# Loading the first batch's q in three long-row parts and putting the tokens back in order later

## The chip, the cores and the metric

The kernel runs on one core of one Trainium2 chip. The metric is the device time of one execution in microseconds (us); the runs before have a median of 262.91 us (three runs, 262.56 to 263.26). The core's engines are PE (TensorE, with its weight loads shown apart as PEld), DVE (VectorE), ACT (ScalarE), POOL (GpSimd) and SP, which here only issues DMAs. Each engine works through its own list of instructions in order and waits on semaphores for the others.

## The reference

There are two blocks, one after the other. The first is a linear attention over sketched features, for 4 batches, 4 heads, 1088 tokens and 32 dimensions:

```python
def phi(x):
    a = np.einsum('rd,bhsd->bhsr', S1, x)          # r = 8
    b = np.einsum('rd,bhsd->bhsr', S2, x)
    return np.einsum('bhsi,bhsj->bhsij', a, b).reshape(*x.shape[:-1], r * r)
q_p, k_p = (phi(q), phi(k))
kv = np.einsum('bhsf,bhsd->bhfd', k_p, v)
z = np.sum(k_p, axis=2)
num = np.einsum('bhsf,bhfd->bhsd', q_p, kv)
den = np.einsum('bhsf,bhf->bhs', q_p, z)[..., None] + 1e-06
attn_out = num / den                               # -> x[b, token, 128], heads side by side
```

The second is a mixture of 4 attention experts over x. A gate picks the best two experts of each token (`w_gate`), each expert does causal attention with its own `wq`, `wk`, `wv`, `wo` (64 wide), and the two results are added with softmax weights of the gate.

Two things matter for the change. The sums `kv` and `z` run over all tokens, so the order of k and v is free as long as both have the same one. q is different: row s of `num` belongs to token s, and the second block is causal, so x has to stand in token order.

## The kernel before

**An order written out by hand.** The kernel declares about 1,280 jobs (`job(...)`), each with the engines it may run on, what it reads and makes, and the buffers that it holds. `ORDER` is one list of job numbers; a letter picks one of two engines (`b` for the second), and a choice of "-" drops the job (unused dummies). `Plan.run` emits the jobs in this order, so each engine's instructions and each DMA queue come in this order, and buffers of a pool are handed out as the list goes: a job that takes a buffer waits until the buffer's former users are through. PSUM has four buffers of two banks, `pair0` to `pair3`, for all work of TensorE. The numbers of estimated microseconds in the jobs don't act at run time.

**The first batch's front.** `prepare(0, ...)` and `attend_rows` make x of batch 0; the later batches go through `attend_turned`, in the shadow of the batch before them.

- k and v of batch 0 come in long rows: partition (head, t) gets 34 adjacent tokens, t counts 32 of them (`load_k`, `load_v`). SP and ACT issue half of k each; SP issues v in four parts.
- q of batch 0 comes by head (`by_head`, line 436): four loads, two on SP and two on ACT. Partition t of a head holds the tokens t, 32 + t, 64 + t and so on, so each piece of a row is one token of 128 bytes. Column block c of 32 columns holds the tokens 32c to 32c + 31.
- DVE turns 32 x 32 blocks (`turn_k` line 484/488, `turn_q` line 494, q in pieces of 384 and 704 columns), so that the dimensions lie on partitions. Both pieces of q wait for all four loads.
- TensorE multiplies 128 tokens at a time with the sketch table `SD` (`project`, line 562); `low` (a copy by ACT or DVE, line 193 as all copies) and `lift` (DVE, line 574) join the two parts of the result, and `multiply` (DVE or POOL, line 580) forms the 64 feature products of each head.
- `spread v` (ACT and POOL, line 193) sets v beside a column of ones. `sums` (TensorE, line 619) adds k's features times v over all tokens, and `keep sums` (ACT) copies the result.
- `turn qf` (`turn_features`, TensorE, line 666) transposes q's features, 18 blocks of 128 x 128 in four jobs of 6, 4, 4 and 4 blocks, each into its own pair. `keep qf` (`keep_features`, ACT, line 193, `fp<-pair`) copies each to `qpT`, in the order in which it stands in PSUM.
- `numer` (TensorE, line 692) multiplies 64 tokens at a time with the sums, `divide` (DVE, lines 699 to 701) divides, `turn x` (TensorE, line 707) and `keep x` (ACT) give x with its 128 columns on partitions.
- `sketch k1` (TensorE, line 523) is the beginning of batch 1 and stands between the numerators.

Then follow the gate (`logits` line 884, `turn logits` line 888, `choose a` and `choose b` lines 911 to 927, `turn choice`, `widen`, masks by DMA through DRAM for the later groups of tokens), the queries (line 1066), `base` (ACT) and `pick` (DVE, line 1079), and the scores (line 1104), which `take` (DVE), `exp` (ACT), `weigh` (POOL) and `turn A` (DVE) pass on to the sums over values (line 1180). `features k1` (line 537) are products of batch 1 on POOL or DVE.

**Dummies.** Pairs of matmuls on a zero tile (line 250) keep TensorE busy before there is work; seven such jobs are in the list.

The lines that the change touches most, as they are:

```python
for y in range(y0, y1):
    z = y - y0
    nc.tensor.transpose(plan[t][:, z // w, 128 * (z % w) : 128 * (z % w) + 128], f[:, y], ident)
...
copy(e, plan[qpT][:, 128 * y0 : 128 * y1], plan[t][:, 0, 0 : 128 * (y1 - y0)])
```

Block y holds the features of two heads (y % 2) for the 128 tokens y // 2.

Of the kernel before, what the change touches and what calls it, by code (L numbers as in the profile page):

```python
# [21 lines left out]
0 1 2 3 4 78 79 83 15a 80 45 21a 48 46 10a 81 90 53b 52b 91 54b 50 25b 18a 49 55b 5b 12a 14a 51 82 84 87 85 86 94 64  # L22
63 95b 96 27a 57 56 58 92 99 93 98b 100a 65 104 97a 101 400 89b 66a 108 103a 88a 105a 114 68 69 106 102b 70 109a 401
115 71a 110 116a 117a 107a 113a 402 399 118 124 111a 112a 59 60 120 61 406 119a 410 125a 122 405 121a 126 67 403 409
127 413 123a 414 128 408 415 134 129a 130 62 407 135 154 131 72 74 73 75 417a 419a 132 155 77 133a 136 404 137a 412
160 161 418a 140 187 138 162 163 156 158 170 188 76 157 693 192a 159 171 175 47 164 165a 176 692 191a 416a 166 189
167a 178 190 691 145 421 177 420 193 141 694 194 411 195 196 197 179 216 230 209 217 182 172 701 422a 183 218 231 198a
424 423 425 428a 223 139 219a 202 173 232 210 233a 427b 184 199 220 174a 221 180 426b 211 702 429 224 203 234 253 222
212b 254 213 185 258a 326 41b 257a 181 431 144 39b 225 255 204 235 186a 256 153 28b 236 430 200 214 226b 215 432 327
149 143 330a 331a 259 205a 142 227 329 700 438 228 168 260 433 148 332 201 328 268 698 229 206 169a 276 434 275 24b  # L30
439 207 283 699 333 277 284 208 269 261 435a 278 270 300 299 285 262 286 436a 287a 237 440 696 279b 442a 437 301 238
9b 705 695 280 441a 288 263 443 264a 708 706 302 152 281 239 303b 240a 271b 241a 289 242a 272 444 709a 282 265 304 245
244 445a 290 704 359 358 712a 273 351 446a 274 350 305 306 707a 266 147 243a 292 710a 366 713a 360 291 367 26b 267 352
361 293 369 362a 11b 353 342 343 38b 294 711a 987 246 697 151 368 363 370 464 295a 296 297 344 345 714 715 371 298 465
# [81 lines left out]
def kernel(  # L116
# [14 lines left out]
    nc = tc.nc  # L131
# [291 lines left out]
    def prepare(b, rank):  # L423
# [42 lines left out]
        if early:  # L466
            for x in range(H):
                job(f"load q{b}.{x}", ("SP", "ACT")[x % 2], 0.7, lambda e, x=x: by_head(nc.scalar if e == "ACT" else nc.sync, plan[qin], q, x),
                    lead, ("qin", b, 0), [qin], landing=0.95, rank=-198.5)
# [921 lines left out]
```

## Time and profile before

| What | us |
|---|---|
| Median of three runs | 262.91 |
| The profiled execution, as timed | 263.49 |
| Its span in the profile | 261.8 |
| PE busy | 254.9 |
| DVE busy | 208.4 |
| POOL busy | 157.5 |
| ACT busy | 105.6 |

All times in the profile count from the start of the span. The profile is of one execution; it is timed 1.7 us longer than its span, and 0.58 us above the median of the runs shown. A row of the timeline gives start, duration of the group, engine, line, operation, what it writes and reads, how many, and in brackets the idle time of its engine before it with what ended it. Busy time of PE includes the dummies, and its matmuls overlap, so differences between starts tell better than durations how long a group holds the engine. TensorE multiplies float32 in two passes, each of which is one row of the count; a transpose is one pass. The granted clock of TensorE was full throughout.

### The profile page before, as it was taken

Reading aid. Unit: us, or ns where it says so; the run is one execution under the profiler, and the core shown is the slowest. Engines: PE = TensorE matmul, PEld = TensorE weight load, DVE = VectorE, ACT = ScalarE, POOL = GpSimd, SP = SyncE. Lnnn points to the kernel's source line nnn. Section 1 sums busy time; section 2 is a strip of 40 time slices with the busy share of each in tenths; the row PEclk is TensorE's granted clock in tenths of the full one; section 3 lists DMA queues with packets and bytes.
Section 4 is the critical chain, followed back from the end, with each engine's and each line's share of the span. In section 5 each row is a group of like instructions: output and inputs, shape, how many; then the busy total and the mean of one; then the engine's idle time right before and its main releaser. Section 6 shows DMA issues by size and latency. Waiting matters only on the chain.

```text
span 261.8 us, 9228 instructions
## 1 busy us (share of the span) xinstructions
PE 254.9 (97%) x3811; PEld 192.2 (73%) x3811; DVE 208.4 (80%) x529; ACT 105.6 (40%) x279; POOL 157.5 (60%) x266
## 2 busy tenths in 40 slices
PE   7899999999999999999999999999999999999995
PEld 2787666646958887665897986666689875589994
DVE  5778999999998996998887497998994388893442
ACT  3453354757242225532814044635514215723120
POOL 5546776899578716597467682366273842542642
PEclk9999999999999999999999999999999999999999
DMA  7978689891467275906044685003370379240012
GB/s 149 212 122 186 112 207 168 158 146 20 73 135 166 67 184 114 148 4 183 3 84 83 143 167 120 4 3 90 93 120 4 96 141 238 47 96 3 5 30 59
DMA packets 87739, 27.35 MB, mean 104 GB/s; under 512 B 58576, under 2 KB 87056, under 8 KB 87696
## 3 DMA queue, kind: packets, MB, share of 16 engines
q1 hardware_dynamic: 85184, 26.15, 50.7%
q10 hardware_dynamic: 2512, 0.61, 1.0%
q8 instruction: 30, 0.49, 0.8%
q14 instruction: 13, 0.11, 0.2%
HBM read 22.22 MB, written 4.52 MB: 102 GB/s over the span
## 4 chain that ended last, share of the span: by engine, by line
PE 84%; DMA 8%; DVE 5%; POOL 1%; issue 1%; SPq 0%; ACT 0%; DVEq 0%; POOLq 0%; ACTq 0%
PE pair L1180 28%; PE pair L1104 24%; PE pair L1066 9%; PE pair L1301 7%; DMA mb<-md 4%; PE pair L1251 3%; PE pair L523 2%; PE pair L827 2%; DMA in<-in_q_dram 2%; DMA w<-in_v_dram 2%; PE pair L627 2%; DVE w L1116 1%; PE pair L1277 1%; DVE fp L805 1%; PE pair L619 1%; PE pair L692 1%
## 5 line engine op out<-in xcount | busy, mean ns | idle before, releaser
L1147 POOL TENSOR_SCALAR w<-w,rs,sh 128x256 f32<-128x256 f32 (+14 forms) x68 | 56.8, 840 | 34.4 <-DVE rs L1143 32.8
L1104 PE MATMUL pair<-xT,qs 128*128 128x320 f32 (+9 forms) x216 | 74.0, 478 | 0.4 <-DVE qs L1079 0.4
L1132 ACT ACTIVATE w<-w,mx 128x64 f32<-128x64 f32 (+15 forms) x68 | 52.4, 772 | 45.8 <-DVE mx L1116 40.6
L1116 DVE CUSTOM_DVE_ANT_0 w<-pair,mask 128x64 f32<-128x64 f32 (+14 forms) x68 | 48.3, 723 | 15.4 <-PE pair L1104 13.0
L1104 PEld LDWEIGHTS pair<-xT,qs 128*128 128x128 f32 x216 | 38.8, 190 | 25.9 <-issue 11.1
L1152 DVE STREAM_TRANSPOSE AT<-w 128x320 f32<-128x320 f32 (+15 forms) x68 | 51.2, 762 | 3.4 <-POOL w L1147 3.0
L1180 PEld LDWEIGHTS pair<-AT,xra 32*128 32x128 f32 x1136 | 41.6, 185 | 4.6 <-issue 2.0
L1180 PE MATMUL pair<-AT,xra 32*128 32x160 f32 (+5 forms) x1136 | 44.9, 303 | 0.0
L1207 POOL TENSOR_TENSOR agg<-agg,mb 128x768 f32<-128x768 f32 (+1 forms) x22 | 34.0, 1559 | 3.4 <-DVE agg L1203 2.0
L1066 PE MATMUL pair<-xT,Mq 128*128 128x384 f32 (+1 forms) x96 | 34.0, 475 | 0.0
L193 ACT COPY agg<-pair 128x384 f32<-128x384 f32 (+1 forms) x31 | 13.2, 463 | 45.5 <-PE pair L1180 44.0
L1180 PEld LDWEIGHTS pair<-AT,xrb 32*128 32x128 f32 x752 | 26.4, 185 | 2.4 <-issue 2.2
L1180 PE MATMUL pair<-AT,xrb 32*128 32x160 f32 (+5 forms) x752 | 28.0, 289 | 0.0
L1140 POOL TENSOR_SCALAR rs<-zs 128x1 f32<-128x1 f32 x32 | 6.8, 214 | 34.0 <-ACT w L1132 23.5
L1066 PEld LDWEIGHTS pair<-xT,Mq 128*128 128x128 f32 x96 | 17.3, 190 | 10.3 <-issue 3.2
L1079 DVE COPY_PREDICATED qs<-mb,pair 128x768 f32<-128x768 uint16 (+1 forms) x24 | 23.1, 962 | 1.5 <-ACT qs L193 0.3
L537 POOL TENSOR_TENSOR fp<-w 128x576 f32<-128x576 f32 x19 | 22.6, 1209 | 1.6 <-DVE w L527 1.1
L1301 PEld LDWEIGHTS pair<-Mo,agg 128*128 128x128 f32 x168 | 20.6, 192 | 2.4 <-issue 0.5
L1301 PE MATMUL pair<-Mo,agg 128*128 128x128 f32 x168 | 21.4, 277 | 0.0
L193 ACT COPY qs<-pair 128x384 f32<-128x384 f32 (+1 forms) x21 | 9.2, 463 | 19.5 <-PE pair L1066 14.2
L1203 DVE COPY_PREDICATED agg<-mb,pair 128x384 f32<-128x384 uint16 (+1 forms) x24 | 12.7, 557 | 4.8 <-ACT agg L193 4.4
L1132 ACT ACTIVATION_READ_ACCUMULATOR w<-w,mx 128x1 f32 x68 | 12.8, 189 | 0.0
(179 smaller groups left out, 297.2 us busy)
## 6 DMA issues: line engine op xcount, KB each, us to landing
xra<-xd SPq DMA_DIRECT2D x16, 192.0 KB, 5.2
xrb<-xd SPq DMA_DIRECT2D x16, 192.0 KB, 5.4
xrc<-xd SPq DMA_DIRECT2D x16, 160.0 KB, 5.0
mb<-md SPq DMA_DIRECT2D x4, 576.0 KB, 7.4
mb<-md SPq DMA_DIRECT2D x4, 480.0 KB, 4.4
mb<-md SPq DMA_DIRECT2D x6, 288.0 KB, 4.3
in<-in_k_dram SPq DMA_DIRECT2D x12, 136.0 KB, 3.4
in<-in_q_dram SPq DMA_DIRECT2D x3, 544.0 KB, 5.6
```

Of the source, the lines that this page charges most:

```text
L193: (nc.scalar.copy if eng == "ACT" else VEC[eng].tensor_copy)(o, i)
L537: VEC[e].tensor_tensor(out=f, in0=a[:, :, None, R : 2 * R].to_broadcast([128, j1 - j0, R, R]), in1=a[:, :, 0:R, None].to_broadcast([128, j ...
L1066: nc.tensor.matmul(plan[ps[x]][:, y, 0:w], Mq[:, ((1, 2), (0, 3))[x][y]], plan[xT][:, 64 * t0 : 64 * t1], start=True, stop=True)
L1079: nc.vector.copy_predicated(chosen(), rows(c), rows(plan[ps[x]]))
L1104: nc.tensor.matmul(plan[p][:, y, 0 : c1 - c0], plan[qs][:, 128 * t : 128 * t + 128], plan[xT][:, c0:c1], start=True, stop=True)
L1116: nc.vector.tensor_tensor_reduce(out=o, in0=src, in1=msk, scale=-1.0, scalar=mx[:, b, i, x - 1 : x] if x else 3e38, op0=ALU.add, op1=ALU.m ...
L1132: nc.scalar.activation(out=a, in_=a, func=ACTF.Exp, bias=mx[:, b, i, last : last + 1], scale=-1.0, accum_out=zs[:, b, i : i + 1])
L1147: nc.gpsimd.tensor_scalar(out=a, in0=a, scalar1=rs[:, b, i : i + 1], scalar2=plan[("sh", b)][:, i : i + 1], op0=ALU.mult, op1=ALU.mult)
L1152: nc.vector.transpose(dst[:, 0 : keys // 32, t], plan[A][:, 0:keys].rearrange("p (j s) -> p j s", s=32))
L1180: nc.tensor.matmul(plan[Vk[g // 2]][:, g % 2, lo : 32 * nt], plan[(f"xr{j // 12}", b)][rows, j % 12], a[rows, j, lo:], start=(j == 0), sto ...
L1207: nc.gpsimd.tensor_tensor(out=a, in0=a, in1=plan[mb][:, 2 * x : 2 * x + 2, 0:w], op=ALU.mult)
L1301: nc.tensor.matmul(plan[p][0:m, 0, 128 * x : 128 * x + 128], plan[agg][:, e, 128 * x : 128 * x + m], Mo[:, e], start=(e == 0), stop=(e == ...
```

## The change

Three things change.

1. **q of batch 0 is loaded in long rows, in three parts.** The parts have 384, 512 and 192 tokens (column blocks 0 to 12, 12 to 28, 28 to 34). In each part, partition (head, t) gets 12, 16 or 6 adjacent tokens, so the rows of the DMA are 1536, 2048 and 768 bytes. SP issues the first and the last, ACT the second. The turn of the first 384 columns waits for the first part alone.
2. **The copies of the turned features restore the order.** In a part of n blocks, column 32c + t now holds token n·t + c of the part. `turn_features` puts the blocks of the two pairs of heads into the two banks of the pair, and `keep_features` writes element (c, t) to place n·t + c: neighbours in PSUM land n elements (12, 16 or 6) apart in `qpT`. The last of the four copies moves 384 instead of 512 elements. `numer` reads its 64 tokens from the new layout.
3. **The front of the order list is new**, up to about a third of the jobs; the last 833 jobs emitted are the same ones in the same order. One load fewer shifts the job numbers by one.

```diff
+        qparts = ((0, 12), (12, 28), (28, 34))
+
+        def load_part(eng, c0, c1):
+            eng.dma_start(out=plan[qin][:, D * c0 : D * c1],
+                          in_=q[b][:, 32 * c0 : 32 * c1].rearrange("h (t c) d -> h t (c d)", t=32))
+
         if early:
-            for x in range(H):
-                job(f"load q{b}.{x}", ("SP", "ACT")[x % 2], 0.7, lambda e, x=x: by_head(nc.scalar if e == "ACT" else nc.sync, plan[qin], q, x),
-                    lead, ("qin", b, 0), [qin], landing=0.95, rank=-198.5)
+            for x, c in enumerate(qparts):
+                job(f"load q{b}.{x}", ("SP", "ACT")[x % 2], 0.45, lambda e, c=c: load_part(nc.scalar if e == "ACT" else nc.sync, *c),
+                    lead, ("qin", b, min(x, 1)), [qin], landing=(c[1] - c[0]) / 15, rank=-198.5)
...
-                [("qin", b, 0)], ("qT", b, x), [qin, qT], ...
+                [("qin", b, x if early else 0)], ("qT", b, x), [qin, qT], ...
...
         def turn_features(y0, y1, t):
             f = plan[fps["q"]].rearrange("p (y f) -> p y f", f=128)
-            w = (y1 - y0) // (2 if y1 - y0 > 4 else 1)
             for y in range(y0, y1):
-                z = y - y0
-                nc.tensor.transpose(plan[t][:, z // w, 128 * (z % w) : 128 * (z % w) + 128], f[:, y], ident)
+                c = 128 * (y // 2 - y0 // 2)
+                nc.tensor.transpose(plan[t][:, y % 2, c : c + 128], f[:, y], ident)
 
         def keep_features(e, y0, y1, t):
-            if y1 - y0 > 4:
-                w = 64 * (y1 - y0)
-                copy(e, plan[qpT][:, 128 * y0 : 128 * y1].rearrange("p (a y) -> p a y", a=2), plan[t][:, :, 0:w])
-            else:
-                copy(e, plan[qpT][:, 128 * y0 : 128 * y1], plan[t][:, 0, 0 : 128 * (y1 - y0)])
+            c0, c1 = 2 * y0, min(2 * y1, C)
+            a0, a1 = [c for c in ((0, 12), (12, 28), (28, 34)) if c[0] <= c0 < c[1]][0]
+            o = plan[qpT].rearrange("p (m s) -> p m s", m=2)[:, :, 32 * a0 : 32 * a1].rearrange("p m (t c) -> p m c t", t=32)
+            copy(e, o[:, :, c0 - a0 : c1 - a0], plan[t][:, :, 0 : 32 * (c1 - c0)].rearrange("p m (c t) -> p m c t", t=32))
...
         def numer(x0, x1, t):
-            f = plan[qpT].rearrange("p (y s) -> p y s", s=128)
+            f = plan[qpT].rearrange("p (m s) -> p m s", m=2)
...
-                    rows = slice(64 * u, 64 * u + 64)
-                    nc.tensor.matmul(plan[t][rows, z // 6, c : c + 2 * (D + 1)], f[:, y, rows],
+                    lo = min(64 * (y - y % 2 + u), S - 64)
+                    nc.tensor.matmul(plan[t][64 * u : 64 * u + 64, z // 6, c : c + 2 * (D + 1)], f[:, y % 2, lo : lo + 64],
```

The new order at the front, engine by engine, as far as the two lists differ in ways that the prediction speaks of (the names are those of the jobs, with the batch and the part behind them):

| Engine | Before | After |
|---|---|---|
| PE | six dummies, project k0, a dummy, project k0+, repeat S2, project q0, q0+, sums 0.0, turn w0, w1, sums 0.1, turn w2, turn qf 0.0, 0.3, 0.1, 0.2, numer 0.0, sketch k1, turn x 0.0, numer 0.2, 0.1, logits 0.0 | six dummies, project k0, q0, k0+, repeat S2, a dummy, project q0+, turn w0, w1, sums 0.0, 0.1, turn w2, turn qf 0.0, 0.1, 0.3, 0.2, numer 0.0, sketch k1, turn x 0.0, numer 0.2, 0.1, logits 0.0 |
| DVE | turn k0.0, k0.1, spread3, low k0, lift k0, turn q0.0, q0.1, multiply k0.0, lift k0+, multiply k0+.1, lift q0, q0+, four q products | turn k0.0, diagonal3, turn k0.1, turn q0.0, spread3, low k0, lift k0, multiply k0.0, turn q0.1, low k0+, lift k0+, multiply k0+.1, lift q0, q0+, four q products, keep sums 0.1 |
| ACT | ... low k0+, keep S2, spread v0, low q0, q0+, keep w, keep sums 0.0, 0.1, keep qf 0.0, 0.3, 0.1, 0.2, keep x 0.0 | ... low q0, keep S2, spread v0, low q0+, keep sums 0.0, keep w, keep qf 0.0, 0.1, 0.2, 0.3, keep x 0.0 |
| POOL | ... pick8, rep16, multiply k0.1, spread v1, multiply k0+.0, gate order, onehot, rep4, features k1.1, .3, .2, ... mask, features k1.0 | ... rep4, pick8, rep16, multiply k0.1, spread v1, multiply k0+.0, mask, gate order, onehot, features k1.1, .3, .2, ... (features k1.0 on DVE) |
| SP | S, k0.0, two q loads, four v loads, w1, w0, w2, four k1 loads | S, k0.0, q0.0, v0.1, q0.2, three v loads, w0, w1, w2, four k1 loads |

On DVE, behind the gate, the new list has choose b, features k1.0, pick, turn choice, pick, maximum where the old one has choose b, turn choice, maximum, pick, pick. Sketch k1 accumulates in two pairs: before in those that turn qf 0.3 and 0.1 used, now in those of turn qf 0.1 and 0.2, in both lists the second and the third copy of ACT. Behind the first scores, the order of scores, weighs and masks of batch 0 differs up to the first queries of batch 1; one of the two copies `keep x 1` goes from ACT to DVE, and two `keep V` copies go the other way.

98 lines of the change are left out of this document (49 added, 49 removed).

## The prediction

> **What bounds the kernel now.** I read the page first: the busy times and the engines of the chain that ended last.
>
> ```profile
> span 261.8 us, 9228 instructions
> PE 254.9 (97%) x3811; PEld 192.2 (73%) x3811; DVE 208.4 (80%) x529; ACT 105.6 (40%) x279; POOL 157.5 (60%) x266
> PE 84%; DMA 8%; DVE 5%; POOL 1%; issue 1%; SPq 0%; ACT 0%; DVEq 0%; POOLq 0%; ACTq 0%
> ```
>
> TensorE is the bound, and its jobs stand in a fixed order. The end can come sooner only by TensorE idle time that disappears, and later by idle time that is added. So the second view is TensorE's timeline (start, duration, idle time before it and who ended that).
>
> ```profile
> 6.67 1.13 PE L562 MATMUL pair<-SD,in 128*128 128x128 f32 x8 [0.70 <-DVE in L484]
> 7.63 0.59 PE L250 MATMUL pair<-idle 128*128 128x512 bf16 x2
> 8.07 1.28 PE L562 MATMUL pair<-SD,in 128*128 128x128 f32 x10
> 9.28 0.63 PE L362 MATMUL pair<-ident,rep 32*128 32x32 f32 x4
> 9.83 2.27 PE L562 MATMUL pair<-SD,in 128*128 128x128 f32 x18
> 12.97 1.12 PE L619 MATMUL pair<-vp,fp 128*64 128x33 f32 x32 [0.86 <-POOL vp L193]
> 14.03 0.87 PE L390 MATMUL pair<-ident,AT 128*128 128x128 f32 x6
> 14.83 1.36 PE L619 MATMUL pair<-vp,fp 128*64 128x33 f32 x40
> 16.12 2.18 PE L666 MATMUL pair<-ident,fp 128*128 128x128 f32 x18
> 18.23 0.92 PE L692 MATMUL pair<-kvz,fp 128*64 128x66 f32 x24
> 19.09 1.60 PE L523 MATMUL pair<-in,SK 32*32 32x288 f32 x64
> 20.62 0.55 PE L707 MATMUL pair<-ident,w 128*128 128x128 f32 x3
> 21.09 1.63 PE L692 MATMUL pair<-kvz,fp 128*64 128x66 f32 x48
> 22.65 0.53 PE L884 MATMUL pair<-xT,wg 128*32 128x192 f32 x8
> ...
> 29.61 2.29 PE L627 MATMUL pair<-vp,fp 128*64 128x33 f32 x72
> 32.28 1.89 PE L1104 MATMUL pair<-xT,qs 128*128 128x64 f32 x8 [0.38 <-DVE qs L1079]
> 52.37 2.18 PE L827 MATMUL pair<-fp,kvr 32*32 32x288 f32 x64 [0.33 <-DVE w L527]
> ```
>
> Real work starts at 6.67. From there to the end three waits stand out: 0.86 for the spread v, 0.38 for the first picks, 0.33 for the second batch's sketch. The first is the prize, since almost nothing can be lost after it. Next, what the other engines do in the front.
>
> ```profile
> 5.81 0.71 DVE L484 STREAM_TRANSPOSE in<-in 128x512 f32<-128x512 f32 x1 [0.30 <-DMA in<-in_k_dram]
> 7.84 0.42 DVE L193 COPY w<-pair 128x256 f32<-128x256 f32 x1 [0.98 <-PE pair L562]
> 8.66 1.37 DVE L494 STREAM_TRANSPOSE in<-in 128x384 f32<-128x384 f32 x2
> 8.80 1.07 POOL L580 TENSOR_TENSOR fp<-w 128x512 f32<-128x512 f32 x1 [1.61 <-DVE w L574]
> 11.09 1.83 POOL L193 COPY vp<-w 64x1024 f32<-64x1024 f32 x1 [1.22 <-DMA w<-in_v_dram]
> 14.80 1.88 DVE L580 TENSOR_TENSOR fp<-w 128x512 f32<-128x512 f32 x3
> 14.94 0.80 ACT L193 COPY AT<-pair 128x768 f32<-128x768 f32 x1 [2.31 <-PE pair L390]
> 17.03 2.27 ACT L193 COPY fp<-pair 128x768 f32<-128x768 f32 x4 [0.36 <-PE pair L666]
> ```
>
> The chain of waits gives the landings behind them: q's first load from 1.87 to 6.40, v's last one at 10.94.
>
> ```profile
> 1.87 4.53 DMA in<-in_q_dram
> 6.42 4.52 DMA w<-in_v_dram
> ```
>
> **The change, part by part.**
>
> *Three long-row loads of q.* The turn of q waits behind other DVE work until 8.66, so an earlier q alone buys nothing. It lets the new list put the turn's first piece into DVE's idle 0.98, and projections of q ahead of those of k's second half. The first part stands in the same place of SP's queue as the load that landed at 6.40, and the turn wants it at 6.52, when k's turn ends; I count no wait. v stands behind fewer q packets, so it lands at 10.94 at the latest. Its copy on POOL comes behind the 1.07 product that ends at 9.87. With v at or before 9.87 the copy ends at 11.70, with v unchanged at 12.8; TensorE wants it at 12.63 (below). The late end costs 0.2, which I put into the range. SP now issues one v load ahead of q's last part, and the weights and second-batch k later in its queue are wanted only after 12 us.
>
> *The front of the list on TensorE.* I take differences of starts as steps. First k projections 0.96, dummies 0.44, second k projections 1.21, S2 0.55, the 18 q passes 2.27 (0.126 each), sums 1.06 and 1.29, six weight turns 0.80, 18 feature turns 2.11. New order: 6.67 + 0.96 + six q passes 0.76 + 1.21 + 0.55 + dummies 0.44 + twelve q passes 1.51 = 12.10; four weight turns 0.53 gives 12.63; all sums 2.35 gives 14.98; two weight turns 0.27 gives 15.25; feature turns 2.11 gives 17.36. DVE makes the products no sooner (it takes over a copy of k's low half, and gains its idle 0.98 only in part): they end at 14.80 + 1.88 = 16.68 in both, and the second feature turn waits for the third product, 0.2. So the turns end at 17.55 instead of 18.23: 0.68 gained. Nearly all of the 0.86 has gone; what is late next is ACT. POOL makes rep4 and the mask sooner. rep4 stands ahead of what the S2 job reads, which TensorE wants at 9.60; POOL's last product follows v's copy, 11.70 + 1.07 = 12.8, and the second half of the sums wants it at 13.69. Both are covered; without the cover each is at most one such 1.07 late.
>
> *The copies that restore the order.* Each now writes single elements 12, 16 or 6 tokens apart. The kernel has one such copy already: xT of later batches, elements 34 tokens apart. By shape:
>
> ```profile
> L193 ACT COPY xT<-pair 128x512 f32<-128x512 f32 x5 | 5.5, 1156 | 2.9 <-PE pair L827 2.9
> L193 ACT COPY xT<-pair 128x64 f32<-128x64 f32 x3 | 1.1, 351 | 0.0
> L193 ACT COPY fp<-pair 128x512 f32<-128x512 f32 x3 | 1.6, 605 | 0.0
> L193 ACT COPY fp<-pair 128x768 f32<-128x768 f32 x1 | 0.8, 799 | 0.4 <-PE pair L666 0.4
> ```
>
> The same 512 elements from the same kind of pair take 1.156 scattered and 0.605 in a row. The line through 64 and 512 elements gives 1.62 for 768 and 0.93 for the last copy, which has 384 now. The four take 1.62 + 1.16 + 1.16 + 0.93 = 4.87 instead of 2.61. Between these two ends I take the upper, because its row is a scattered copy. [...]
>
> ACT starts the first copy when the weights' copy (0.80, after the last weight turn at 15.4) is done: 16.2. They end at 17.8, 19.0, 20.15 and 21.1 (before: all by 17.03 + 2.27 = 19.30).
>
> *Who waits for them.* The numerators read the halves from other columns in as many passes of the same size: no cost. The first numerator starts at 17.85 and takes 0.86: 18.71. The k1 sketch behind it accumulates in the two pairs that the second and third copies read out: its first 16 passes wait until 19.05, the other 48 until 20.2 and take three quarters of 1.53, so 21.35. Before, these copies were done when it came. Turn of x 0.47, 21.82; two numerators 1.56, 23.38. That answers to 22.65 in the row of the logits: **0.73 late**, the 0.68 spent and as much again.
>
> *To the first scores.* TensorE has the same set of jobs there, so it is free at 31.90 + 0.73 = 32.63. DVE's picks decide:
>
> ```profile
> 23.25 0.17 DVE L699 TENSOR_SCALAR den<-pair 128x12 f32<-128x12 f32 x1
> 23.72 0.56 DVE L701 TENSOR_TENSOR w<-pair,den 128x384 f32<-128x384 f32 x1
> 30.06 2.17 DVE L1079 COPY_PREDICATED qs<-mb,pair 128x768 f32<-128x768 uint16 x2
> L537 DVE TENSOR_TENSOR fp<-w 128x576 f32<-128x576 f32 x5 | 3.9, 802 | 0.8 <-POOL w L801 0.8
> L927 DVE TENSOR_TENSOR c<-c x4: 168/168/1136, 28.6 to 168.7; 128x18 bf16<-128x18 bf16 x3, 128x22 bf16<-128x22 bf16 x1
> 28.50 1.17 POOL L537 TENSOR_TENSOR fp<-w 128x576 f32<-128x576 f32 x1
> ```
>
> A divide takes 1.03 from its first instruction to its end (23.25 to 24.28, the last of three). The two numerators now end near 22.6 and 23.38, so two divides in a row end at 22.75 + 2.06, some 0.57 after 24.28. DVE gets one feature product of batch 1 (0.80) ahead of the picks and sheds a 0.15 maximum. Its L927 took 1.136 once, beside POOL's L537, and 0.168 three times. That POOL product is the one that moves to DVE, so L927 may give back up to 0.97. Picks end at 32.23 + 1.22 = 33.45 or at 32.48. Against 32.63 that is a wait of 0.87 or none; I take 0.38, the present one and near the middle.
>
> *Behind that.* Scores, weighs and masks are reordered up to some 80 us, the rest is unchanged. Bounds: the 0.33 at 52.37 goes, or one wait of a scattered x copy (1.1, which DVE now does once) appears. Nearest is the trace itself, one wait of 0.33: no difference.
>
> **Sum**: +0.73. Against the profiled execution's 263.49 that is 264.2; it lies 0.58 above the median 262.91, so **263.6** for the median. 0.3% is 0.79 us, about what a measurement can tell from no change.
>
> **Rivals.**
>
> *Copies as cheap as before (the other side).* If strides of 24 to 64 bytes cost nothing, the copies hide behind 17.55, and sketch, numerators and divides stay 0.68 early. TensorE is free for the scores at 31.90 - 0.68 = 31.22, and the picks end at 32.23 - 0.68 + 0.65 - 0.97 = 31.23: the 0.38 wait goes too, some 0.95 saved, **262.0**. For it: no row has these strides. Against: the row of 136 bytes. It decides from where the four copies take under some 3.2 us together.
>
> *Late picks.* DVE holds the extra product and L927 stays long: wait 0.87, total 1.22, 264.1; with a second wait of 1.1 for the scattered x copy on DVE, **265.2**. For it: DVE is 80% busy over the whole span and is the releaser of both late waits. Against: POOL is relieved by the same product.
>
> *The loads change nothing.* v lands at 10.94 still: 0.2 more, 263.8; the second copy of v then stays in front of the sums.
>
> **How the numbers follow.** My forecast, the third rival's 0.2 taken in, 0.46: it lies between 262.9 and 264.4 by the unknown wait at the scores, so about half of it is beyond the 0.3%. Cheap copies 0.22, nearly all faster. Late picks with or without the second wait 0.32, all slower. Faster 0.20, same 0.26, slower 0.54. The range 261.7 to 265.4 runs from cheap copies with a slightly earlier k to late picks with the second wait; the forecast's own is 262.9 to 264.4.
>
> **What would show it.** The four feature copies at 1.6, 1.16, 1.16 and 0.93; the sums at about 12.6 with no wait; the k1 sketch with a gap of a microsecond, released by ACT; the logits at 23.4; a short wait at the first score; L927 short. Wrong if the copies take 0.6 to 0.8, if the turns end later than 17.6 because the products come late, or if a new wait over 1 us stands between 33 and 80 us.

## The result, and the profile after

The changed kernel takes 271.3 us (median of six, 268.5 to 273.1) beside 262.7 for the kernel before: 1.030 times, with a 95% interval of 1.023 to 1.036. The ratio leaves out the slowest execution, which is over 1.5% above the fastest and counts as slow. My forecast was 263.6, with a range up to 265.4.

One remark is needed to read the numbers: executions of the changed kernel differ more than those of the kernel before, and in four of the six the mean granted clock of TensorE is below 0.99: it is halved for a while, as a second profile shows further down. Time and mean granted clock of the six are 268.53 us at 1.000, 268.73 at 0.998, 271.08 at 0.985, 271.44 at 0.986, 272.54 at 0.980 and 273.12 at 0.979. The profile after is of the first, at full clock; its span is 266.8 us (before: 261.8). So 5.0 us have to be found in the profile, and up to 4.6 us more come in the executions with a lower clock.

Rows of TensorE's timeline of the changed kernel (others between them are left out, here and in the fences below):

```profile
6.35 1.13 PE L568 MATMUL pair<-SD,in 128*128 128x128 f32 x8 [0.22 <-POOL pick L344]
10.57 2.05 PE L568 MATMUL pair<-SD,in 128*128 128x128 f32 x16 [3.09 <-DVE in L500]
14.01 1.60 PE L568 MATMUL pair<-SD,in 128*128 128x128 f32 x12 [0.29 <-DVE in L500]
15.98 1.12 PE L625 MATMUL pair<-vp,fp 128*64 128x33 f32 x32
17.41 1.36 PE L625 MATMUL pair<-vp,fp 128*64 128x33 f32 x40 [0.31 <-POOL fp L586]
21.46 0.92 PE L696 MATMUL pair<-kvz,fp 128*64 128x66 f32 x24 [0.34 <-ACT fp L193]
26.64 0.53 PE L888 MATMUL pair<-xT,wg 128*32 128x192 f32 x8
33.60 2.29 PE L633 MATMUL pair<-vp,fp 128*64 128x33 f32 x72
35.82 1.58 PE L1108 MATMUL pair<-xT,qs 128*128 128x64 f32 x8
```

The 0.86 in front of the sums is gone, but 3.09 us stand in front of the projections of q, which I had put at 7.63. The sums begin at 15.98, not at 12.63; the logits at 26.64, not at 23.38. Nearly the whole difference to my forecast is there ahead of the sums. Who was late shows on DVE:

```profile
5.49 0.71 DVE L490 STREAM_TRANSPOSE in<-in 128x512 f32<-128x512 f32 x1
9.94 0.58 DVE L500 STREAM_TRANSPOSE in<-in 128x384 f32<-128x384 f32 x1 [3.74 <-DMA in<-in_q_dram]
13.04 0.91 DVE L500 STREAM_TRANSPOSE in<-in 128x704 f32<-128x704 f32 x1 [0.68 <-DMA in<-in_q_dram]
```

On POOL:

```profile
14.57 1.06 POOL L193 COPY vp<-w 64x1024 f32<-64x1024 f32 x1 [1.28 <-DMA w<-in_v_dram]
```

And in the chain of waits (start, duration, what):

```profile
5.00 9.43 DMA w<-in_v_dram
```

DVE has turned k and then waits 3.74 us for the first part of q, though that load was issued at 1.88. v's last load is issued 1.4 us earlier than before and lands at 14.43, 9.43 us after its issue instead of 4.52. The loads are slow. How slow shows in the windows (busy time of the five engines, granted clock, DMA share of 16 engines, GB/s) of the changed kernel:

```profile
8.00:9.00 1.00, 0.00 (x0) 0.00 (x0) 0.00 (x0) 0.00 (x0) 0.00 (x0) 1.00 0.28 88
9.00:10.00 1.00, 0.00 (x0) 0.00 (x0) 0.06 (x1) 0.00 (x0) 0.00 (x0) 1.00 0.26 98
```

The same windows of the kernel before:

```profile
8.00:9.00 1.00, 1.00 (x11) 0.97 (x10) 0.97 (x3) 0.00 (x0) 0.20 (x1) 1.00 1.11 239
9.00:10.00 1.00, 1.00 (x9) 0.84 (x8) 1.00 (x3) 0.43 (x2) 0.87 (x1) 1.00 1.21 217
```

While everything waits for q, the DMA engines are busy 0.28 of 16, 4.5 engines by that share, and move 88 GB/s; before, the share is 1.11 and 1.21 in the same two windows. Each part of q is one load whose outermost dimension is the four heads (`"h t (c d)"`; h and t can't be merged, since a part is only a piece of a head). That gave theory A: the loads run on four DMA engines, and v stands behind q's packets on those four. The windows give the mean share of all 16 engines, not which engine moves which packet, and a share of 1.11 can't be a count of busy engines; so the four are my estimate from the 0.28 and the four heads, and v's place behind q is an argument. The rivals were theory B, in which the long rows or the places in the queues are slow, and theory C, in which the new list costs the time.

### The profile page after: what moved, and what is told of

Its sections match the earlier page's. It is cut to its first block, busy times and chain, and to the rows that moved or that the text cites. A ratio compares the mean times of both kernels' runs of the same rounds, so it can differ in the third digit from the quotient of the medians.

```text
span 266.8 us, 9223 instructions
## 1 busy us (share of the span) xinstructions
PE 256.7 (96%) x3811; PEld 192.0 (72%) x3811; DVE 207.9 (78%) x528; ACT 107.2 (40%) x284; POOL 156.8 (59%) x262
## 3 DMA queue, kind: packets, MB, share of 16 engines
HBM read 22.22 MB, written 4.52 MB: 100 GB/s over the span
## 4 chain that ended last, share of the span: by engine, by line
PE 91%; DMA 4%; SPq 1%; ACT 1%; issue 1%; POOL 1%; DVE 1%; POOLq 0%; ACTq 0%
PE pair L1184 29%; PE pair L1108 26%; PE pair L1070 11%; PE pair L1305 7%; DMA w<-in_v_dram 4%; PE pair L1255 3%; PE pair L529 3%; PE pair L633 2%; PE pair L831 2%; PE pair L1281 1%; PE pair L671 1%; ACT fp L193 1%; PE pair L882 1%; POOL fp L586 1%; SPq L443 1%
## 5 line engine op out<-in xcount | busy, mean ns | idle before, releaser
L1151 POOL TENSOR_SCALAR w<-w,rs,sh 128x256 f32<-128x256 f32 (+16 forms) x68 | 56.9, 842 | 35.4 <-DVE rs L1147 33.7
L1108 PE MATMUL pair<-xT,qs 128*128 128x384 f32 (+10 forms) x216 | 73.7, 478 | 0.0
L1120 DVE CUSTOM_DVE_ANT_0 w<-pair,mask 128x64 f32<-128x64 f32 (+15 forms) x68 | 48.5, 725 | 14.9 <-PE pair L1108 12.7
L1156 DVE STREAM_TRANSPOSE AT<-w 128x256 f32<-128x256 f32 (+15 forms) x68 | 51.0, 761 | 4.3 <-POOL w L1151 4.1
L193 ACT COPY agg<-pair 128x384 f32<-128x384 f32 (+1 forms) x33 | 14.2, 464 | 45.3 <-PE pair L1184 43.2
L543 POOL TENSOR_TENSOR fp<-w 128x576 f32<-128x576 f32 x18 | 21.4, 1211 | 3.6 <-DVE w L533 3.2
```

The source lines that it names most:

```text
L193: (nc.scalar.copy if eng == "ACT" else VEC[eng].tensor_copy)(o, i)
L543: VEC[e].tensor_tensor(out=f, in0=a[:, :, None, R : 2 * R].to_broadcast([128, j1 - j0, R, R]), in1=a[:, :, 0:R, None].to_broadcast([128, j ...
L1108: nc.tensor.matmul(plan[p][:, y, 0 : c1 - c0], plan[qs][:, 128 * t : 128 * t + 128], plan[xT][:, c0:c1], start=True, stop=True)
L1120: nc.vector.tensor_tensor_reduce(out=o, in0=src, in1=msk, scale=-1.0, scalar=mx[:, b, i, x - 1 : x] if x else 3e38, op0=ALU.add, op1=ALU.m ...
L1151: nc.gpsimd.tensor_scalar(out=a, in0=a, scalar1=rs[:, b, i : i + 1], scalar2=plan[("sh", b)][:, i : i + 1], op0=ALU.mult, op1=ALU.mult)
L1156: nc.vector.transpose(dst[:, 0 : keys // 32, t], plan[A][:, 0:keys].rearrange("p (j s) -> p j s", s=32))
```

## The experiments

### The outermost dimension alone, on the new list

```diff
             eng.dma_start(out=plan[qin][:, D * c0 : D * c1],
-                          in_=q[b][:, 32 * c0 : 32 * c1].rearrange("h (t c) d -> h t (c d)", t=32))
+                          in_=q[b].rearrange("h (t c) d -> (h t) (c d)", c=C)[:, D * c0 : D * c1])
```

> The changed kernel with the same three loads of the same bytes and the same rows (1536, 2048 and 768 bytes), on the same queues in the same places, but cut so that the outermost dimension is 128 rows instead of four heads: partition (head, t) holds 34 adjacent tokens, and each part takes some columns of all of them. The copies stay as they are, so the tokens of batch 0 come out in another order; the work is the same. Theory A (four heads outermost: only four DMA engines): q's first part has landed and its turn starts by 7 us instead of 9.94, v's last load lands by 11 instead of 14.43, the sums begin at 12.5 to 13.5 instead of 15.98, no idle stretch of TensorE over 1 us, the granted clock at 1.0 in nearly all executions, median 263 to 264.5 as I forecast for the change. Theory B (long rows or the places in the queues) and theory C (the list): 266 or more.

Measured: 265.39 us (264.80 to 265.51), 1.0076 times the kernel before [1.0047, 1.0104], and a granted clock of 0.999 to 1.0 in all four. The first turn of q starts at 6.98, by DVE's timeline:

```profile
6.98 0.54 DVE L500 STREAM_TRANSPOSE in<-in 128x384 f32<-128x384 f32 x1
```

TensorE's timeline of the same run:

```profile
7.20 2.92 PE L568 MATMUL pair<-SD,in 128*128 128x128 f32 x24 [1.69 <-DVE in L490]
12.91 2.29 PE L625 MATMUL pair<-vp,fp 128*64 128x33 f32 x72
15.41 2.15 PE L671 MATMUL pair<-ident,fp 128*128 128x128 f32 x18
17.90 0.92 PE L696 MATMUL pair<-kvz,fp 128*64 128x66 f32 x24 [0.33 <-ACT fp L193]
23.06 0.53 PE L888 MATMUL pair<-xT,wg 128*32 128x192 f32 x8
30.03 2.29 PE L633 MATMUL pair<-vp,fp 128*64 128x33 f32 x72
32.25 2.65 PE L1108 MATMUL pair<-xT,qs 128*128 128x64 f32 x12
```

The rows of the loads have the same lengths, and they stand in the same places of the same queues. The cut differs, and with it which tokens a row holds and so where it starts in memory; the two experiments that cut by heads keep the rows of the changed kernel and show that this isn't the cause. The wait for q has gone, POOL copies v's last part at 10.96 without a wait for its load (14.57 behind a wait of 1.28 in the changed kernel), and sums, numerators and logits are at 12.91, 17.90 and 23.06 where I had 12.63, 17.85 and 23.38. Theory B falls, and theory C falls as the cause of the large loss as long as q comes early; what the list costs when q comes late is shown by the list alone. The time lies between what I gave theory A (up to 264.5) and what I gave the others (266 and more), and 1.0 us above the forecast's own range (up to 264.4); the last experiment tells why.

### Two heads outermost

```diff
-            eng.dma_start(out=plan[qin][:, D * c0 : D * c1],
-                          in_=q[b][:, 32 * c0 : 32 * c1].rearrange("h (t c) d -> h t (c d)", t=32))
+            for h in (0, 2):
+                eng.dma_start(out=plan[qin][32 * h : 32 * h + 64, D * c0 : D * c1],
+                              in_=q[b, h : h + 2, 32 * c0 : 32 * c1].rearrange("h (t c) d -> h t (c d)", t=32))
```

> The changed kernel with each part of q in two loads of two heads each (outermost dimension two instead of four; same bytes, rows, queues and order, three issues more). Theory A (the outermost dimension sets the number of DMA engines): q moves on two engines at half the rate; in the changed kernel q's 544 KB took from 4.0 to 12.0 us, so here until about 20, q's first part is turned at 14 to 17 us instead of 9.94, and the median is 274 to 282. Theory B (large transfers or rows as such, whatever the number of engines): smaller loads are no later, 268 to 272.

Measured: 273.72 us, 1.041 times [1.037, 1.044]. DVE's row:

```profile
14.61 0.58 DVE L501 STREAM_TRANSPOSE in<-in 128x384 f32<-128x384 f32 x1 [8.34 <-DMA in<-in_q_dram]
```

One window:

```profile
8.00:9.00 1.00, 0.00 (x0) 0.00 (x0) 0.00 (x0) 0.00 (x0) 0.00 (x0) 1.00 0.13 50
```

A DMA share of 0.13 is 2.1 of 16 engines. The first part of q is turned at 6.98 with 128 rows outermost, at 9.94 with four heads and at 14.61 with two, though the loads with two are half the size. The time lies just below my 274 to 282: the turn came at the early end of the 14 to 17 that I gave it. Theory A holds as far as these runs go: half the outermost dimension gives about half the share (0.13 for 0.28) and 50 GB/s for 88. That two engines and four stand behind the shares remains my estimate; no view shows it.

### The loads alone, on the old list

The kernel before with the three part loads and nothing else; then the same with the rows as in the first experiment (the edit shown is that of the first of the two):

```diff
+        def load_part(eng, c0, c1):
+            eng.dma_start(out=plan[qin][:, D * c0 : D * c1],
+                          in_=q[b][:, 32 * c0 : 32 * c1].rearrange("h (t c) d -> h t (c d)", t=32))
...
-            for x in range(H):
-                job(... by_head(nc.scalar if e == "ACT" else nc.sync, plan[qin], q, x), ...
+            for x, c in enumerate(((0, 12), None, (28, 34), (12, 28))):
+                job(... c and load_part(nc.scalar if e == "ACT" else nc.sync, *c), ...
```

> The kernel before with nothing changed but q's loads: the three part loads (the first on SP, the second first on ACT, the third on SP) in place of the four by head. The copies stay as they were, so the tokens of batch 0 come out in another order; the work is the same. Theory A (four DMA engines): the turn of q moves from 8.66 to about 10 us, v's last load lands near 14 instead of 10.94, the sums begin 2.5 to 3.5 us late, and the median is 265 to 267. Theories B in its queue form and C (place in the new queue, the list): within 0.5 us of before, since the list is the old one.

> The kernel before with its own list, in which q's four loads by head are replaced by three loads of 128 rows each (some columns of all rows, as above; the first on SP, the second first on ACT, the third on SP). The copies stay as they were, so the tokens of batch 0 come out in another order. It differs from the run with the three part loads on the old list (268.1) in the cut of the loads alone. Theory A: q's turn starts before 8.66, v lands before 10.94, so the 0.86 wait for v shrinks and the median is 261.8 to 263; the 5 us between the two runs are the four DMA engines. Theory B (long rows make the loads late): 265 or more.

Measured: 268.09 us (1.021 [1.016, 1.026]) with four heads outermost, above my 265 to 267, and 263.10 us (1.0001 [0.998, 1.002]) with 128 rows, just above my 261.8 to 263. TensorE's rows of the one with four heads:

```profile
13.79 2.93 PE L566 MATMUL pair<-SD,in 128*128 128x128 f32 x12 [3.31 <-DVE in L498]
16.65 1.15 PE L623 MATMUL pair<-vp,fp 128*64 128x33 f32 x32
```

And of the one with 128 rows:

```profile
12.16 1.13 PE L623 MATMUL pair<-vp,fp 128*64 128x33 f32 x32
```

On the old list, too, the cut costs 5 us: neither the new list nor the copies are needed for a loss of this size. It isn't the cut's wait alone, though: the four executions with four heads outermost have clocks of 0.981 to 0.994, and the 12 passes in the row above take 2.93 at a granted clock of 0.50 (14 to 16 us) where they take 1.50 at 1.00 in the run with 128 rows on the new list. And fast long-row loads on the old list bring nothing, although the wait for v is gone (12.16 without a gap). The prize that I had named first is worth nothing measurable by itself.

### One head at a time

```diff
-            eng.dma_start(out=plan[qin][:, D * c0 : D * c1],
-                          in_=q[b][:, 32 * c0 : 32 * c1].rearrange("h (t c) d -> h t (c d)", t=32))
+            for h in range(H):
+                (nc.sync, nc.scalar)[h % 2].dma_start(out=plan[qin][32 * h : 32 * h + 32, D * c0 : D * c1],
+                              in_=q[b, h, 32 * c0 : 32 * c1].rearrange("(t c) d -> t (c d)", t=32))
```

> The changed kernel with each of the three parts of q cut into four loads of one head (32 rows each, t outermost; heads 0 and 2 on SP, 1 and 3 on ACT). Bytes, row lengths, places in the list, copies and order stay. Theory A (each part load has the four heads outermost and is spread over only four DMA engines, so q's first part is late and v's packets stand behind q's on these four): the turn of q's first part starts before 7.5 us instead of 9.94, v's last load lands before 12.5 instead of 14.43, the sums begin by 14 instead of 15.98, and the median is 263 to 265. Theory B (the long rows, or the place of the loads in the queues, make q late): the turn still waits beyond 9 us and the time stays at 267 to 269. Theory C (the new list is what costs): the loads come early and the time stays above 266.

Measured: 266.89 us (1.015 [1.011, 1.018]), above the 263 to 265 that I gave theory A: by the terms that I had set (loads early, time above 266) this is the outcome of theory C. The loads are early (q's first turn is at 6.57, and POOL's copy of v's last part, at 12.73, waits for no load), but ACT issues the last four of its six loads from 4.48 to 7.11, and makes part of the sketch table behind its issues. ACT's timeline:

```profile
4.48 2.63 ACTq L470 DMA_DIRECT2D in<-in_q_dram  x4
7.29 0.67 ACT L193 COPY SD<-SK 32x32 f32<-32x32 f32 x3
```

TensorE's:

```profile
8.05 4.33 PE L569 MATMUL pair<-SD,in 128*128 128x128 f32 x24 [2.58 <-ACT SD L193]
```

TensorE starts at 8.05 for that reason, and takes 4.33 for what took 2.92 above, with a granted clock of 0.50 from 7.6 to 11.0. The experiment mends one thing and breaks another, so alone it would not have decided. A better version has two parts of 384 and 704 tokens, eight loads, and no more of them on ACT than before the change; it computes everything that the changed kernel computes:

> The changed kernel mended: q in two parts (384 and 704 tokens) by head, with t (32) outermost: four loads of 32 rows of 1536 bytes on SP, then four of 2816 bytes, two on SP and two on ACT, ahead of v. ACT issues no more loads than before the change. The copies restore the order (12 and 22 tokens apart). Theory A: q's first turn by 7.5 us, v's last load by 12, no throttled stretch, and a time as in the run with 128 rows outermost (265.4): 264.8 to 266. It doesn't reach the kernel before, since the copies and the list stay. Theory B: 267 or more.

Measured: 266.43 us (1.014 [1.010, 1.018]), just above my 264.8 to 266. q's first turn is at 7.15 and the mean clock at 0.997 to 1.0, but POOL waits 1.03 for v's last load, behind eight loads of q, and copies it from 11.54, and the sums wait 0.36 for v and 0.82 for a product on POOL behind v. So it is 1 us above the run with 128 rows, and doesn't beat the kernel before.

### The list alone

The new list with the loads and copies of before:

> The changed kernel's list with the loads of before (four loads by head with rows of 128 bytes: head 0 on SP, heads 1 and 3 on ACT, head 2 on SP behind v's first load) and copies of the features in the order in which they stand. Theory A (few DMA engines): q's turn starts near 8.6 us as before, the second projections of k are held back to about 9.3 by the list, the sums begin near 14.3, and the median is 263 to 264.5. Theory C (the list): above 266.

Measured: 267.98 us (1.018 [1.015, 1.020]), where I had expected 263 to 264.5; by the terms that I had set (above 266) this is the outcome of theory C, so the list alone, with the loads of before, loses too. In this queue order q's first turn waits 3.04 for q's loads and is at 9.55 (8.66 before, without such a wait), the new list keeps the second projections of k behind those of q, and the idle time is followed by a slow stretch. TensorE's row:

```profile
10.18 2.73 PE L568 MATMUL pair<-SD,in 128*128 128x128 f32 x16 [2.39 <-DVE in L500]
```

Some windows:

```profile
11.00:12.00 1.00, 1.00 (x9) 1.00 (x8) 0.97 (x3) 0.32 (x1) 0.67 (x1) 0.68 0.54 87
12.00:13.00 1.00, 1.00 (x6) 0.78 (x4) 0.85 (x2) 0.00 (x0) 0.94 (x2) 0.50 0.00 0
18.00:19.00 1.00, 1.00 (x30) 0.79 (x28) 1.00 (x2) 0.00 (x0) 0.38 (x1) 0.91 0.01 0
```

The granted clock (third number from the right) is 0.50 from about 11.4 to 18.2, and the mean clock is 0.986 to 0.994 in all six executions, so a part of this loss is the clock too. The new list therefore has no cover for a late q: the old one has ten passes of k and a dummy there. With q early it costs little, as the next experiment shows. So a late q is what the two losses have in common: the cut makes it late on either list, and the new list loses even to a turn of q that is 0.9 us late.

### The price of the copies

The run with 128 rows outermost, with the four copies writing in the order of PSUM:

```diff
-            a0, a1 = [c for c in ((0, 12), (12, 28), (28, 34)) if c[0] <= c0 < c[1]][0]
-            o = plan[qpT].rearrange("p (m s) -> p m s", m=2)[:, :, 32 * a0 : 32 * a1].rearrange("p m (t c) -> p m c t", t=32)
-            copy(e, o[:, :, c0 - a0 : c1 - a0], plan[t][:, :, 0 : 32 * (c1 - c0)].rearrange("p m (c t) -> p m c t", t=32))
+            o = plan[qpT].rearrange("p (m s) -> p m s", m=2)
+            copy(e, o[:, :, 32 * c0 : 32 * c1], plan[t][:, :, 0 : 32 * (c1 - c0)])
```

> As the run before, but the four copies of the turned features write them in the order in which they stand in PSUM (the step that restores the order is left out, so the tokens of batch 0 come out in another order). By my prediction the restoring costs 2.2 us of ScalarE and 0.7 to 1.4 of the end: 0.7 to 1.4 us less than the run before, 262 to 263. Rival (the copies lie beside other work, or cost what they did): within 0.3 of the run before.

Measured: 263.87 us, 1.0023 times the kernel before [0.9999, 1.0046], so 1.5 us less than with the restoring copies, where I had expected 0.7 to 1.4. The groups of ACT's copies in the changed kernel (count, busy us, mean ns, idle before):

```profile
L193 ACT COPY fp<-pair 128x512 f32<-128x512 f32 x2 | 2.0, 1084 | 0.0
L193 ACT COPY fp<-pair 128x768 f32<-128x768 f32 x1 | 1.5, 1532 | 0.0
L193 ACT COPY fp<-pair 128x384 f32<-128x384 f32 x1 | 0.9, 912 | 0.0
```

The logits on TensorE's timeline of this run:

```profile
21.89 0.53 PE L887 MATMUL pair<-xT,wg 128*32 128x192 f32 x8
```

Logits at 23.06 with and 21.89 without the restoring: 1.17 in the front, with the sums at 12.91 and 12.90.

### Dummies in the idle stretch

The changed kernel with six more dummies between the first projections of k and of q:

> The changed kernel with six more dummy pairs between the first projections of k and those of q, where TensorE stood idle for 3.09 us; they take about 6 x 0.44 = 2.64 of it. Theory A1 (the idle stretch lets the clock of TensorE be lowered for a while in some executions): the undisturbed time stays at about 268.5, but all executions are near it, with a mean granted clock of 0.998 to 1.0, so the median comes to 268 to 269 instead of 271.3. Rival A2 (the lower clock in some executions has another cause): times still go from 268 to 273 with clocks down to 0.98.

Measured: 268.13 us (267.55 to 270.75; 1.022 [1.018, 1.025]); the mean clock is 0.998 to 1.0 in five executions of six and 0.991 in the one of 270.75. That one is the profiled one, and there the clock falls at about 18.5 us, not behind the wait for q but behind two waits of 0.66 and 0.62 in the sums:

```profile
18.00:19.00 1.00, 0.89 (x22) 0.89 (x24) 1.00 (x2) 0.00 (x0) 0.95 (x2) 0.75 0.27 57
```

To see the clock in the changed kernel itself, it was profiled once more:

> The changed kernel, unchanged, for a second profile and more executions. Theory A1 (the idle 3.09 us lets the clock be halved in some executions): most executions lie between 270 and 273.5 with a mean granted clock of 0.978 to 0.988, some at 268.5 with 0.998 to 1.0, none between by more than the clock explains; if the profiled one is a slow one, its rows show a clock of 0.50 that begins between 9 and 14 us and lasts 3.4, 6.8 or 10.2 us, the matmuls in it take up to twice as long, and the front of the list ends 2 to 5 us later than in the first profile. Rival A2 (the spread comes from the landings of the loads): the clock's rows are at 1.00 in the front, and the loads land later.

Measured: 268.09, 268.66, 269.96 and 270.53 us, at 0.991, 0.993, 0.992 and 0.986; median 269.3, 1.023 times [1.018, 1.029]. The second profile (268.66) has the slow stretch. TensorE's row:

```profile
9.98 3.35 PE L568 MATMUL pair<-SD,in 128*128 128x128 f32 x16 [2.14 <-DVE in L500]
```

The windows:

```profile
10.00:11.00 1.00, 1.00 (x7) 1.00 (x8) 0.93 (x3) 0.00 (x0) 0.21 (x1) 0.75 0.65 186
12.00:13.00 1.00, 1.00 (x7) 1.00 (x5) 0.00 (x0) 0.00 (x0) 0.71 (x1) 0.50 0.54 130
13.00:14.00 1.00, 1.00 (x6) 0.78 (x5) 0.90 (x2) 0.00 (x0) 0.00 (x0) 0.55 0.30 73
```

The clock is at 0.50 from about 10.5 to 13.9, and 16 passes take 3.35 instead of 2.05. So the slow stretch is there, and with dummies in the idle time the clock stays up in five executions of six (A1, nearly). But it isn't the whole spread: this execution is no slower than the first. Its q was turned 0.59 earlier, and of the two waits of the first profile behind that (0.29 for q's second part, 0.31 in the sums) it has none, so by the turns of the features it is level (18.93 and 18.98). And 268.09 was reached at 0.991. My "most executions at 0.978 to 0.988" missed; over all ten executions of the changed kernel the clock is from 0.979 to 1.0.

### The kernel before again, and a load moved behind

In the runs on the new list TensorE stands idle in the second batch's numerators without a releaser (0.79 in the run with 128 rows); in the profile of before it doesn't. The trace has packets of 16 KB on queue 8, which it calls instructions; the fifth starts at 52.0 us in that run, at TensorE's 677th matmul, and at 49.9 us, the 611th, in the profile of before. Two runs on that:

> The run with 128 rows outermost on the new list, and the third batch's load of q (544 KB) issued behind four more fetches of x (issued at 45.74 us there). In that run TensorE stood idle for 0.79 us in the middle of the second batch's numerators without a releaser, and its instruction packet of 16 KB on queue 8 started at 52.0 us, at its 677th matmul, while in the profile of before it started at the 611th and nothing stood idle there. Theory D (the packet waits behind the load of q): without the load ahead of it the packet starts near the 611th matmul, the idle 0.79 goes, the median is 264.2 to 264.8. Rival E (the packet's place has another cause): the idle time stays, 265.1 to 265.7.

> The kernel before, unchanged, for a second profile. Theory D (the load of q stands behind the instruction packet in that list): again no idle time inside the second batch's numerators, and the packet near the 611th matmul. Rival (it is chance which of them comes first): an idle stretch of 0.5 us or more there now.

Measured: 265.39 us with the load moved behind, the same as without, with the same idle 0.79 behind the same 52nd matmul of the numerators. Theory D falls. TensorE's timeline in the second profile of the kernel before (263.14 us, span 261.4):

```profile
6.24 1.13 PE L562 MATMUL pair<-SD,in 128*128 128x128 f32 x8
11.87 1.12 PE L619 MATMUL pair<-vp,fp 128*64 128x33 f32 x32 [0.19 <-POOL vp L193]
28.53 2.29 PE L627 MATMUL pair<-vp,fp 128*64 128x33 f32 x72
31.09 1.89 PE L1104 MATMUL pair<-xT,qs 128*128 128x64 f32 x8 [0.27 <-DVE qs L1079]
```

It is 1.08 us earlier at the sums of batch 1 (28.53 against 29.61): DVE doesn't wait the 0.30 for k's second half, TensorE starts at 6.24, and the wait for v is 0.19 instead of 0.86. Then it has an idle 0.45 in the numerators, behind their 52nd matmul, and ends 0.4 earlier. So the profile on which I predicted was unusual in two places: a late front, and no idle time later.

Where the idle stretch stands tells what it is. TensorE's numerators of batch 1 in the run with 128 rows, and then in the run with six dummies:

```profile
51.98 2.10 PE L831 MATMUL pair<-fp,kvr 32*32 32x288 f32 x52
54.88 0.69 PE L831 MATMUL pair<-fp,kvr 32*32 32x256 f32 x12 [0.79 <-issue]
```

```profile
57.77 1.92 PE L831 MATMUL pair<-fp,kvr 32*32 32x288 f32 x40
60.37 0.74 PE L831 MATMUL pair<-fp,kvr 32*32 32x288 f32 x24 [0.69 <-issue]
```

Six dummies are twelve matmuls, and the stretch moves from behind the 52nd to behind the 40th; in the other profiles that have it, it is behind the 51st or the 52nd. So it stands at nearly a fixed place of TensorE's list of instructions, whatever is computed there. I read that as TensorE running out of instructions, which no view shows; it has this stretch in all profiles but the first of the kernel before (0.25 to 1.10 us). What delays it stays open.

Taken against this second profile, the changed kernel is 5.07 late at the sums of batch 1 (33.60 against 28.53) and 5.4 at the end of the span; the run with 128 rows 1.50 and 2.4. Matmul for matmul, the run with 128 rows is still 1.5 late at 190 us, 1.9 behind a wait near 194 us, and the remaining 0.5 stands behind the last matmul: from its end to the end of the span it is 3.7 us in this run (260.09 to 263.8) and in the first profile of the changed kernel (263.09 to 266.8), and 3.2 in the two of the kernel before (258.56 to 261.8, and 258.21 to 261.4).

## Why the prediction was wrong, step by step

**Three long-row loads: the step that failed.** I wrote that the first part "stands in the same place of SP's queue as the load that landed at 6.40" and "I count no wait". I priced the load by its place and its bytes, and not by its shape: the load that landed at 6.40 has 32 rows outermost, the new one four heads. The turn came at 9.94 instead of 6.52, v at 14.43 instead of "10.94 at the latest", and the sums 3.35 later than my 12.63. The change of shape stood in the diff, and I gave it no bound from above: the only end for late loads was 0.2. With 128 rows outermost the time is 265.4 instead of 268.5 at full clock, 3.1 us less, and 5 us less on the old list, the clock included.

**The clock, missing.** An idle stretch of 3 us was not among my cases, so neither was a lower clock behind it. Most executions lie above the first profile's, by up to 4.6 us. In the first six the time rises as the mean clock falls; in the four later ones it doesn't do so cleanly, so how much of the spread is the clock stays open.

**The prize, too large.** The 0.86 was that of one execution; in the second profile it is 0.19. That takes 0.67 from the gain of every case. The new list with quick loads and straight copies came to 263.87, 0.5 above the kernel before in that comparison, where my rival of cheap copies had 0.95 below (262.0). Besides, with q in 128 rows k's first half is turned at 5.33 instead of 4.73 (5.27 on the old list), and the new list puts a copy between k's two turns: TensorE starts at 7.20, not at 6.67.

**The order on TensorE was right.** With quick loads there are 5.71 us from the first projection to the sums (mine 5.96), and the turns end at 17.56 (mine 17.55). That the ends agree so well is luck: the sums begin 0.28 later than I had them, and the 0.2 that I counted for the third product isn't there.

**The copies: each was right, the chain of them too long.** I had 1.62, 1.16, 1.16 and 0.93; the four take 1.53, twice 1.08 and 0.91, 4.61 instead of 4.87. But I set them one behind the other, from 16.2 to 21.1, and their records overlap. In ACT's timeline of the run with 128 rows they are through at 20.28:

```profile
16.31 3.97 ACT L193 COPY fp<-pair 128x768 f32<-128x768 f32 x4
```

The row of the kernel before shows the same: four copies in 2.27, whose means add to 2.61. That strides of 48, 64 and 24 bytes (12, 16 and 6 elements) cost what 136 bytes cost (34 elements) was my assumption, and no run that I had then showed it; the changed kernel shows it roughly: 512 elements 64 bytes apart take 1.08 where 512 elements 136 bytes apart took 1.16. A stride of 88 bytes, at the end of this document, doesn't fit.

**The waits for them: right in kind, a little too long.** I had 0.73 late plus the 0.68 spent, 1.41, at the logits; restoring against not restoring is 1.17 there and 1.5 in the medians. The sketch of k1 was to lose 1.11 (2.64 instead of 1.53) and loses 0.73: 64 passes take 2.33 instead of 1.60, with one wait of 0.7 for ACT behind the first 16 and smaller steps, since the copies were through earlier than I had them. The numerators at 17.90 and the logits at 23.06 stand 0.05 and 0.32 from my 17.85 and 23.38; in part that is luck again, with sums that begin 0.28 late and copies that end 0.8 early.

**First scores.** I took a wait of 0.38; there is none (35.82, and 32.25 with quick loads). Two divides from 22.75 end 0.53 behind 24.28, not the 0.57 that I wrote; nothing hangs on it. The long L927 is gone as I thought it might be: 0.168 to 0.175 in all four.

**Behind that, no difference:** true against the second profile up to 190 us (1.5 late at the sums of batch 1 with 128 rows, and 1.5 at 190 us), false against the first, which has no idle time in the second batch's numerators. The 0.5 behind the last matmul I didn't see coming.

The sum itself, +0.73, is a fair account of the kernel that I thought I was reading: that one measures +2.0 [1.2, 2.7]; 0.7 of it is the smaller prize, and 0.5 the end behind the last matmul.

## What to carry over

Price a load by the outermost dimension of its access pattern, not only by bytes, row length and place: here q's first turn came at 6.98 us with 128 rows outermost, at 6.57 and 7.15 with 32 (one head at a time, two parts), at 9.94 with four heads and at 14.61 with two. The cut that left four heads outermost ran at a share of 0.28 of the 16 DMA engines, and v's last load behind it took 9.43 us instead of 4.52. A list that is tuned to tighter loads loses the work that covered a late one (268.0 us with the loads of before), and idle stretches of 2.14 and 2.39 us on TensorE were followed by a granted clock of 0.50 for 3.4 and 6.8 us. Before a wait below 1 us is called the prize, see whether a second profile has it.

## What the runs showed that I had not expected

- The granted clock fell to half for 3.4 or 6.8 us in six of the fourteen profiles. In the second profile of the changed kernel and with the list alone it did so (10.5 to 13.9, and 11.4 to 18.2) after idle stretches of 2.14 and 2.39 us, 0.5 and 1.2 us after TensorE had begun to work again; with one head at a time, with the parts on the old list and with two heads it fell while TensorE stood idle (7.6 to 11.0, 13.3 to 16.7 and 11.6 to 18.5), and with six dummies from 18.5 to 21.9. After the idle 3.09 us in the first profile of the changed kernel it didn't fall at all.
- The length of the idle time alone doesn't tell whether the clock falls: behind 3.09 us and, with 128 rows, behind 1.69 us it stayed at 1.00, behind 2.14 us it fell, and with six dummies it fell behind two waits of 1.28 together. What decides it isn't shown.
- Behind q's loads with four heads outermost v's last load, whose outermost dimension is 32, was late: 9.43 us from issue to landing instead of 4.52 before. Behind q in 128 rows POOL's copy of it, at 10.96, waits for no load.
- The end behind the last matmul is 0.5 us longer in the changed kernel and in the run with 128 rows than in the kernel before (3.7 for 3.2), though the last 833 jobs are the same. Why wasn't tried.
- In the run with two parts, where the last three of the four feature copies write elements 22 apart (88 bytes), the four take 4.95 us from the first's start to the last's end, beside 3.97 with 16, 16 and 6 apart in the run with 128 rows. Why isn't settled.
